# Attention products with v issued as quarter-array matmuls into two PSUM banks, probabilities copied whole, one visit moved by a place

## The chip, the cores and the metric

The kernel runs on one core of a Trainium2 chip. The metric is the device time of one execution in microseconds (us), lower is better; runs of the same program on the same chip are compared by their medians. Engine names are those of the profile: PE is the matrix engine (PEld its weight loads), DVE the vector engine, ACT the scalar engine, POOL the general engine, SP the queue that issues input transfers.

## The reference, cut to what matters

Chunked attention followed by a gated two-layer network:

```python
def _attn_ref(q, k, v, mem_k, mem_v):            # q, k, v: 4 x 8 x 768 x 64, 8 memory keys
    chunk, left_ctx, right_ctx = (32, 16, 8)
    for c in range(S // chunk):
        ...                                       # k_full, v_full: memory + 16 left + 32 own + 8 right = 64 keys
        scores = scale * np.matmul(q_c, k_full.transpose(0, 1, 3, 2))
        scores = scores - np.max(scores, axis=-1, keepdims=True)
        a = np.exp(scores)
        a = a / (np.sum(a, axis=-1, keepdims=True) + 1e-09)
        out[:, :, c_start:c_end] = np.matmul(a, v_full)

def _moe_ref(x, w_gate, w_val, w_out, rms_g):     # x: 3072 x 512, inner width 1536
    rms = np.sqrt(np.mean(x * x, axis=-1, keepdims=True) + 1e-06)
    xn = x / rms * rms_g
    g = xn @ w_gate
    silu = g * (1.0 / (1.0 + np.exp(-g)))
    val = xn @ w_val
    return (silu * val @ w_out)
```

## The kernel before

**Network.** The 3072 tokens are eight blocks of 384. For each block and each of 12 slices of the inner width (`f`), PE makes `pg` (gate, 12 matmuls of 128x128 weights on 384 columns), `pv` (value, 12 of the same) and adds to `po` (output, 9 matmuls on 512 columns). Each operand is split into a high and a low part, so that three matmuls stand for one. ACT and DVE turn `pg` and `pv` into `hh` and `hl`, the high and low part of the inner activations, that `moe_out` of that slice needs: tanh (`silu_a`), `silu_b` (in the first blocks after `gr`, a product of `pg` with the row scale), `moe_m` (`t<-t,pv`), `moe_hh`, `moe_hl`.

**Attention.** It is cut into 32 units: batch, half of the sequence, and a pair of heads. The first eight units, the first two blocks and the preparation of the weights run in a first part whose order is written out by hand (`ORDER`, up to about 150 us). What follows are seven segments: segment 0 finishes block 0 from slice 5 on, segments 1 to 6 do blocks 2 to 7. The other 24 units, twelve pairs, are done inside segments 0 to 5, in visits.

**Visits.** A segment has places ("gaps"): gap 2j stands behind `pg` of its j-th slice, gap 2j+1 behind `pv` of it; then comes `po` of the slice before. `VISITS` says at which gaps the generator `late_steps` advances: "v" is a visit, "n" one step of the norm that closes a block's input, "p" a visit's first half alone. Visit n does, for the pair of before (`old`): the transposes of the probabilities `pT` (`stage_p`, 6 matmuls), their copies to SBUF (`stage_c`; the tiles are named `pt` for even units and `qp` for odd ones, where q and the probabilities share a tile), the products with v (`stage_o`) and the copies into the block's input `xT` with their squares `sq` (`late_r`); for the pair of now (`cur`): the scores `s` (`stage_s2`, 48 small matmuls: 64 rows by 32 columns of the array each), the maximum `mx`, the difference, the exponential (`stage_m`, `stage_e`) and the normalisation `r`, `pe<-pe,r` (`stage_d`); and it issues the loads of the next pair. Every second visit closes a block: `late_n` splits the sum of squares into `sh` (ACT) and `sl` (DVE), and in the next "n" step PE sums them over the partitions (`ssum`). Twelve visits have products with v: two in segment 0 (gaps 5 and 9), two in each of segments 1 to 4 (gaps 5 and 17), and in segment 5 gap 5 and the pair of gaps 17 ("p") and 18.

**Products with v before.** The copies spread each unit's transposed probabilities into a tile twice as wide, zero elsewhere, so that one matmul serves two neighbouring chunks: all 128 rows of the array hold both chunks' keys (`v` of the pair of chunks), 64 columns, and 64 moving columns. That is 12 matmuls a unit, two units one after the other; the first unit's result goes to a bank of the pool `psa` (three banks in turn), the second's to the bank of `pv`. Each unit's copy is made in two halves, by ACT and by DVE.

**What sets the order.** PE's late instructions keep the program's order (`on_pe`). DVE's and ACT's order is set by the framework's scheduler from priorities, and each engine runs its list strictly in that order.

Of the kernel before, what the change touches and what calls it, by code (L numbers as in the profile page):

```python
# [8 lines left out]
F32 = mybir.dt.float32  # L9
# [4 lines left out]
AF = mybir.ActivationFunctionType  # L14
ALU = mybir.AluOpType
# [5 lines left out]
CH = 32  # L21
# [3 lines left out]
P = 128  # L25
NG = H // 2
HT = 384
NT = HT // P
NC = HT // CH
NJ = NC // 2  # L30
# [4 lines left out]
NE = NG * 2  # L35
WP = 2 * KC - LC - RC
KN, VN = NJ * WP, NJ * 2 * D
# [2 lines left out]
YMAX = 0x1DFE / 0x1000 * 2.0 ** -96  # L40


VISITS = (((1, "v"), (5, "v"), (9, "v"), (10, "n"), (11, "n"), (12, "n")),
# [27 lines left out]
def tile_kernel(ctx: ExitStack, tc: tile.TileContext, q, k, v, w_gate, w_val, w_out, rms_g, out):  # L71
    nc = tc.nc
    const = ctx.enter_context(tc.tile_pool(name="const", bufs=1))
    p1 = ctx.enter_context(tc.tile_pool(name="p1", bufs=1))
# [28 lines left out]
    def on_pe(ins):  # L103
        if pinned:
            tc.keep_in_program_order(ins)

    def psum_a(name):
        return psa.tile([P, 512], F32, name=name, tag="at")

    def psum_m(tag, name):  # L110
        return psm.tile([P, 512], F32, name=name, tag=tag)
# [4 lines left out]
    units = [(b, hf, g) for b in range(B) for hf in range(2) for g in range(NG)]  # L116
    st = {}
    pts = [early.tile([P, NT, 4, 2, CH], F32, name=f"pt{i}") for i in range(2)]
    late = {}

    def zeros(t):
        nc.gpsimd.memset(t, 0.0)
        return t

    def late_buffers(i):

        if i:
            t = p1.tile([P, HT + VN], F32, name="qp1", tag="A")
            late["q", 1], late["pt", 1] = t[:, 0:HT], zeros(t[:, HT:])
            late["kv", 1] = p1.tile([P, KN + VN], F32, name="kv1", tag="B")  # L130
        else:
            late["q", 0] = p1.tile([P, HT], F32, name="q0", tag="q")
            late["pt", 0] = zeros(p1.tile([P, VN], F32, name="pt0", tag="wy"))
            late["kv", 0] = p1.tile([P, KN + VN], F32, name="kv0", tag="ws")
        late["pt", i] = late["pt", i].rearrange("p (i a s q) -> p i a s q", i=NT, a=4, s=2)

    def load_qk(u):
        d = st.setdefault(u, {})
# [16 lines left out]

    def pt_of(u):

        return pts[u % 2] if u < NE else late["pt", u % 2]

    def copy(e, out, in_):  # L160
        if e == "a":
            return nc.scalar.copy(out, in_)  # L162
        if e == "g":
            return nc.gpsimd.tensor_copy(out=out, in_=in_)
        return nc.vector.tensor_copy(out=out, in_=in_)  # L165
# [37 lines left out]
    def stage_m(u):  # L203
        stage_ma(u)
        stage_mb(u)
# [20 lines left out]
    def stage_e(u):  # L226
        pe = st[u]["p"]
        nc.scalar.activation(pe, pe, AF.Exp, scale=0.125)

    def stage_d(u):  # L230
        stage_da(u)
        stage_db(u)
# [25 lines left out]
    def stage_p(u, tag=None):  # L258
        d = st[u]
        t = psum_m(tag, f"pT{u}") if tag else psum_a(f"pT{u}")  # L260
        pe = d["p"].rearrange("p j k -> p (j k)")
        for i in range(NT):
            on_pe(nc.tensor.transpose(out=t[:, i * P:(i + 1) * P], in_=pe[:, i * P:(i + 1) * P], identity=ident))  # L263
        d["t"] = t

    def stage_c(u):
        stage_ch(u, 0, "a")
        stage_ch(u, 1, "d")

    def stage_ch(u, hh, e):  # L270
        r = slice(64 * hh, 64 * hh + 64)
        t4 = st[u]["t"][:, 0:HT].rearrange("p (i a q) -> p i a q", i=NT, q=CH)
        copy(e, pt_of(u)[r, :, :, hh, :], t4[r])

    def stage_o(u, tag=None):

        pt, vw = pt_of(u), st[u]["v"]
        o = psum_m(tag, f"o{u}") if tag else psum_a(f"o{u}")
        for j in range(NJ):
            for hh in range(2):  # L280
                on_pe(nc.tensor.matmul(o[64 * hh:64 * hh + 64, j * D:(j + 1) * D], lhsT=vw[:, j, hh],  # L281
                                 rhs=pt[:, j // 2, 2 * (j % 2) + (hh ^ (u % 2 if u >= NE else 0))].rearrange("p c q -> p (c q)"),
                                 start=True, stop=True))
        st[u]["o"] = o[:, 0:HT]

    def late_r(u, x):

        g = units[u][2]
        o = st.pop(u)["o"]
        nc.scalar.copy(x[:, g], o)  # L290
        s = obuf(f"sq{u}")[:, 0:HT]
        nc.scalar.activation(s, x[:, g], AF.Square)
        if g:
            nc.vector.tensor_tensor(out=s, in0=s, in1=late["ss"], op=ALU.add)
        late["ss"] = s

    def late_n(x):

# [191 lines left out]
    def obuf(name):  # L490
        return p3.tile([P, DM], F32, name=name, tag="stg")
# [59 lines left out]
    def last_of(eng):  # L551
        return next(i for i in reversed(nc.cur_bb.bb.instructions) if i.engine == eng.engine)

    late_x = {}

    def late_steps():


        pairs = [(u, u + 1) for u in range(NE, len(units), 2)]
        for n in range(len(pairs) + 1):  # L560
            old = pairs[n - 1] if n else ()
            cur = pairs[n] if n < len(pairs) else ()
            new = pairs[n + 1] if n + 1 < len(pairs) else ()
            for u in old[0:1]:
                if u % NG == 0:
                    late_x["x"] = p1.tile([P, NKT, HT], F32, name="xT", tag="x")
            x = late_x.get("x")
            with tc.high_priority():
                for i, u in enumerate(old):
                    stage_p(u, None if i else "g")  # L570
                for u in old:
                    stage_c(u)
            if not cur:
                yield "p"
            with tc.high_priority():
                if cur:
                    stage_s2(cur)
                for u in cur:
                    stage_m(u)
                for u in cur:  # L580
                    stage_e(u)
                for i, u in enumerate(old):
                    stage_o(u, "v" if cur and i else None)
                for u in old:
                    late_r(u, x)
            norm = late_n(x) if n and n % 2 == 0 else ()
            if norm:
                with tc.high_priority():
                    next(norm)
            with tc.high_priority():  # L590
                for i, u in enumerate(cur):
                    if norm and i:
                        with tc.issue_after(last_of(nc.vector)):
                            stage_d(u)
                    else:
                        stage_d(u)
            for u in new:
                load_qk(u)
            for u in cur if n else ():
                load_v(u)  # L600
            yield "v"
            for _ in norm:
                yield "n"
# [10 lines left out]
    sq = [xq[:, i] for i in range(4)]  # L614
# [68 lines left out]
    def tok_o(n):  # L683
# [10 lines left out]
        P=lambda n: stage_p(n, "o0" if n < NG else None),  # L694
# [4 lines left out]
        g=tok_in("g"), v=tok_in("v"), p=tok_q("g"), q=tok_q("v"),  # L699
        r=tok_r, h=tok_h, i=tok_i, j=tok_j, k=tok_k, l=tok_l, o=tok_o,  # L700
# [5 lines left out]
    for tok in ORDER.split():  # L706
# [4 lines left out]
        e = tok[-1] if tok[1:] and tok[-1].isalpha() else ""  # L711
# [38 lines left out]

    xs = xs01[0]
    todo = late_steps()
    for sg, (blk, f0) in enumerate(segments):
        po = [psm_o(i) for i in range(NT)] if sg else sp["po", 0]
        last = sg == len(segments) - 1
        steps = {} if last else dict(VISITS[min(sg, 2) + (sg == len(segments) - 2)])

        def visit(gap):
            if gap in steps and next(todo, None) not in (steps[gap], None):
                raise AssertionError(gap)  # L760
        for f in range(f0, NF):
            g = moe_in("g", f, xs, last)
            visit(2 * (f - f0))
            out_ = lambda f=f, h=prev: moe_out(f - 1, h, po)
            if f == f0:
                out_ = lambda: None
                if sg == 0:

                    moe_out(NF - 1, prev, po1)
                    with tc.high_priority():  # L770
                        store(1, po1)
            vv = moe_in("v", f, xs, last)
            visit(2 * (f - f0) + 1)
            if f < NF - 1:
                out_()
                prev = moe_h(g, vv, blk)
            elif last:
                out_()
                finish(f, g, vv, po, blk)
            else:  # L780
                with tc.high_priority():
                    t = moe_t(g, vv, blk)
                xs = split_x(late_x["x"], t, out_, lambda h: moe_out(NF - 1, h, po))
        if sg == 0:
            behind.close()
        if not last:
            store(blk, po)
# [65 lines left out]
```

## Time and profile before

| what | value |
|---|---|
| median of 3 runs (lowest, highest) | 708.42 us (708.2, 708.72) |
| the profiled execution: its time, its span | 707.74 us, 705.9 us |
| busy: PE, PEld, DVE, ACT, POOL | 687.4, 636.3, 392.3, 261.4, 6.1 us |
| instructions | 13419 |
| products with v in the visits (L281) | 576 PE records, 12 visits |
| scores in the visits (L200) | 1152 PE records, 12 visits |

The span runs from the first to the last instruction; 1.84 us of the execution lie outside it. A row of the timeline gives the start, the duration, the engine, the line, the operation, `out<-in`, the array tile (rows*columns), the operand's shape and a count of merged records. A matmul's duration is its way through the array; how often matmuls can follow each other is read from the distance of their starts. A matmul on plain fp32 operands leaves two records, one on split operands (`xh`, `wh_g` and the like) one.

### The profile page before, as it was taken

What the parts mean: (1) busy time and instruction counts of PE and PEld (TensorE: products, weight loads), DVE (VectorE), ACT (ScalarE), POOL (GpSimd) and SP (SyncE); (2) the same over time, 40 slices, a digit from 0 to 9 for tenths busy, and PEclk for the clock granted to TensorE, in tenths of its full rate; (3) what the DMA queues carried; (4) which work ended last, traced back from release to release, by engine and by line L of the source; (5) the groups of instructions that cost most, each with busy time, mean ns of one, the idle gap of its engine ahead of it and who ended that gap; (6) DMA issues with size and microseconds to landing.
All of it is one profiled execution on the core that took longest, in us unless ns stands there. A gap on an engine that the chain in (4) does not pass through costs nothing.

```text
span 705.9 us, 13419 instructions
## 1 busy us (share of the span) xinstructions
PE 687.4 (97%) x5702; PEld 636.3 (90%) x5702; DVE 392.3 (56%) x780; ACT 261.4 (37%) x474; POOL 6.1 (1%) x14
## 2 busy tenths in 40 slices
PE   7899999999999999999999999999999999999997
PEld 6798898999989999999999999999999999999996
DVE  6789999857674327552383525735276532552222
ACT  4697987733333113331233313222133311331112
POOL 0010000000000000000000000000000000000000
PEclk8899999999999999999999999999999999999999
DMA  9644644333321103130021303013031100010001
GB/s 319 246 167 137 235 149 139 115 132 109 115 90 51 58 0 105 46 104 1 17 90 45 105 1 89 16 46 105 1 104 46 45 3 0 1 46 1 0 1 46
DMA packets 22620, 55.14 MB, mean 78 GB/s; under 512 B 2464, under 2 KB 6816, under 8 KB 22560
## 3 DMA queue, kind: packets, MB, share of 16 engines
q1 hardware_dynamic: 19824, 49.55, 20.9%
q10 hardware_dynamic: 2736, 4.72, 1.8%
q8 instruction: 45, 0.74, 0.5%
q14 instruction: 15, 0.12, 0.1%
HBM read 47.97 MB, written 6.29 MB: 77 GB/s over the span
## 4 chain that ended last, share of the span: by engine, by line
PE 88%; DVE 5%; ACT 4%; issue 1%; DMA 1%; POOL 0%; SPq 0%; DVEq 0%; ACTq 0%
PE pg L437 27%; PE pv L437 27%; PE po L487 27%; PE o L281 3%; PE pT L263 1%; ACT pt L162 1%; DVE pt L165 1%; DVE qp L165 1%; DMA k<-in_k_dram 1%; ACT ws L392 1%; ACT ws L381 1%; PE s L184 1%; PE ss L622 1%; ACT wy L382 1%; DVE xT L325 1%
## 5 line engine op out<-in xcount | busy, mean ns | idle before, releaser
L437 PE MATMUL pv<-xh,wh_v 128*128 128x384 f32 x384 | 130.1, 339 | 2.1 <-DVE t L458 2.1
L437 PE MATMUL pg<-xh,wh_g 128*128 128x384 f32 x384 | 130.5, 340 | 0.0
L437 PE MATMUL pv<-xh,wl_v 128*128 128x384 f32 x384 | 129.7, 338 | 0.5 <-DVE wl_v L408 0.5
L437 PE MATMUL pg<-xl,wh_g 128*128 128x384 f32 x384 | 129.8, 338 | 0.0
L437 PE MATMUL pg<-xh,wl_g 128*128 128x384 f32 x384 | 129.8, 338 | 0.0
L437 PE MATMUL pv<-xl,wh_v 128*128 128x384 f32 x384 | 129.6, 337 | 0.0
L162 ACT CAST hh<-t 128x384 fp32r<-128x384 f32 x89 | 45.8, 515 | 192.7 <-PE po L487 176.0
L487 PE MATMUL po<-wh_o,hh 128*128 128x512 f32 x285 | 113.9, 400 | 0.7 <-ACT hh L744 0.6
L487 PE MATMUL po<-wh_o,hl 128*128 128x512 f32 x285 | 112.6, 395 | 0.0
L487 PE MATMUL po<-wl_o,hh 128*128 128x512 f32 x285 | 112.3, 394 | 0.0
L455 DVE SCALAR_TENSOR_TENSOR t<-t,pg 128x384 f32<-128x384 f32 x72 | 39.9, 554 | 105.8 <-ACT t L451 105.7
L467 DVE TENSOR_TENSOR hl<-t,hh 128x384 fp32r<-128x384 f32 x89 | 49.5, 556 | 85.7 <-ACT hh L162 85.6
L458 DVE TENSOR_TENSOR t<-t,pv 128x384 f32<-128x384 f32 x95 | 52.7, 554 | 71.5 <-PE pv L437 70.2
L451 ACT ACTIVATE t<-pg 128x384 f32<-128x384 f32 x72 | 35.5, 493 | 120.2 <-PE pg L437 120.2
L437 PEld LDWEIGHTS pg<-xh,wh_g 128*128 128x128 f32 x384 | 72.3, 188 | 4.1 <-DVE gr L446 0.4
L437 PEld LDWEIGHTS pg<-xl,wh_g 128*128 128x128 f32 x384 | 72.3, 188 | 3.6
L437 PEld LDWEIGHTS pv<-xh,wh_v 128*128 128x128 f32 x384 | 72.0, 188 | 3.6 <-DVE t L458 1.8
L437 PEld LDWEIGHTS pv<-xh,wl_v 128*128 128x128 f32 x384 | 72.0, 188 | 0.8 <-DVE wl_v L408 0.8
L437 PEld LDWEIGHTS pg<-xh,wl_g 128*128 128x128 f32 x384 | 72.2, 188 | 0.0
L437 PEld LDWEIGHTS pv<-xl,wh_v 128*128 128x128 f32 x384 | 72.1, 188 | 0.1
L487 PEld LDWEIGHTS po<-wh_o,hl 128*128 128x128 f32 x285 | 53.6, 188 | 13.6 <-DVE hl L745 0.6
L487 PEld LDWEIGHTS po<-wh_o,hh 128*128 128x128 f32 x285 | 53.5, 188 | 10.7 <-ACT hh L744 1.6
(110 smaller groups left out, 717.2 us busy)
## 6 DMA issues: line engine op xcount, KB each, us to landing
kv<-in_v_dram SPq DMA_DIRECT2D x24, 384.0 KB, 5.6
kv<-in_k_dram SPq DMA_DIRECT2D x24, 312.0 KB, 4.2
out_dram<-ob ACTq DMA_DIRECT2D x18, 256.0 KB, 2.1
ws<-in_moe_w_gate_dram SPq DMA_DIRECT2D x4, 1024.0 KB, 4.9
ws<-in_moe_w_val_dram SPq DMA_DIRECT2D x4, 1024.0 KB, 5.0
ws<-in_moe_w_out_dram SPq DMA_DIRECT2D x4, 1024.0 KB, 5.0
q<-in_q_dram SPq DMA_DIRECT2D x20, 192.0 KB, 3.1
vw<-in_v_dram SPq DMA_DIRECT2D x8, 384.0 KB, 7.3
```

Of the source, the lines that this page charges most:

```text
L162: return nc.scalar.copy(out, in_)
L165: return nc.vector.tensor_copy(out=out, in_=in_)
L184: nc.tensor.matmul(s[a:a + CH, o:o + KC], lhsT=d["q"][r, c * CH:c * CH + CH], rhs=k[r], start=True, stop=True)
L263: on_pe(nc.tensor.transpose(out=t[:, i * P:(i + 1) * P], in_=pe[:, i * P:(i + 1) * P], identity=ident))
L281: on_pe(nc.tensor.matmul(o[64 * hh:64 * hh + 64, j * D:(j + 1) * D], lhsT=vw[:, j, hh], rhs=pt[:, j // 2, 2 * (j % 2) + (hh ^ (u % 2 if u ...
L325: nc.vector.scalar_tensor_tensor(out=x[:, kt], in0=x[:, kt], scalar=rg[:, kt:kt + 1], in1=r, op0=ALU.mult, op1=ALU.mult)
L437: on_pe(nc.tensor.matmul(ps[:, 0:HT], lhsT=weight(a, n, f, kt), rhs=xs[c][:, kt], start=kt == 0 and i == 0, stop=kt == NKT - 1 and i == 2))
L451: nc.scalar.activation(t, g, AF.Tanh, scale=0.5)
L455: nc.vector.scalar_tensor_tensor(out=t, in0=t, scalar=1.0, in1=g, op0=ALU.add, op1=ALU.mult)
L458: nc.vector.tensor_tensor(out=t, in0=t, in1=vv, op=ALU.mult)
L467: nc.vector.tensor_tensor(out=hl, in0=t, in1=hh.bitcast(F32), op=ALU.subtract)
L487: on_pe(nc.tensor.matmul(po[i], lhsT=h[a][:, i * P:(i + 1) * P], rhs=weight(c, "o", f), start=f == 0 and n == 0, stop=f == NF - 1 and n == 2))
```

## The change

Four edits that go together:

- `stage_o2` in place of two `stage_o`: each product with v is cut into the two chunks that shared the rows. A matmul has 64 rows (one chunk's keys), 64 columns and 32 moving columns; chunks on the upper rows write the bank `oe` (from `psa`), those on the lower rows the bank `oo`. A pair of units takes 48 matmuls in place of 24, the four quarters of the array in turn.
- `stage_c` copies a unit's transposed probabilities in one piece of 128x384, ACT for the even unit, DVE for the odd one; the tiles are half as wide and the two zeroing instructions on POOL go.
- `late_r` copies the pair's results from the two banks, each copy holding every second chunk of both units, into `xT`, then makes both squares.
- The third visit of segment 0 moves from gap 9 to gap 8, the norm steps from 10, 11, 12 to 9, 10, 11. Which bank the first transposes and `oo` take now follows the gap (`lent["even"]`): at an odd gap `pg`'s and `pv`'s as before, at an even one `pv`'s and `pg`'s.

```diff
-VISITS = (((1, "v"), (5, "v"), (9, "v"), (10, "n"), (11, "n"), (12, "n")),
+VISITS = (((1, "v"), (5, "v"), (8, "v"), (9, "n"), (10, "n"), (11, "n")),
...
     def stage_c(u):
-        stage_ch(u, 0, "a")
-        stage_ch(u, 1, "d")
+        copy("da"[u % 2 == 0], late["pt", u % 2], st[u]["t"][:, 0:HT])
...
+    def stage_o2(pair, tag):
+
+        st["o2"] = o2 = [psum_a(f"oe{pair[0]}"), psum_m(tag, f"oo{pair[0]}") if tag else psum_a(f"oo{pair[0]}")]
+        for j in range(NJ):
+            for n, u in enumerate(pair):
+                pt = late["pt", u % 2].rearrange("p (j e q) -> p j e q", j=NJ, e=2)
+                for cp in range(2):
+                    r, o = slice(64 * cp, 64 * cp + 64), (NJ * n + j) * CH
+                    for hh in range(2):
+                        on_pe(nc.tensor.matmul(o2[cp][64 * hh:64 * hh + 64, o:o + CH], lhsT=st[u]["v"][r, j, hh],
+                                               rhs=pt[r, j, hh ^ u % 2], start=True, stop=True))
...
+        xc = x[:, g:g + 2].rearrange("p g (j c q) -> p g j c q", c=2, q=CH)
+        for cp in range(2):
+            nc.scalar.copy(xc[:, :, :, cp], o2[cp][:, 0:HT].rearrange("p (g j q) -> p g j q", g=2, q=CH))
...
-                    stage_p(u, None if i else "g")
+                    stage_p(u, None if i else "gv"[lent["even"]])
...
-                for i, u in enumerate(old):
-                    stage_o(u, "v" if cur and i else None)
-                for u in old:
-                    late_r(u, x)
+                if old:
+                    stage_o2(old, "vg"[lent["even"]] if cur else None)
+                    late_r(old, x)
```

PE at the visit of gap 5 in segment 0, before: the last score rows (`s`), the two units' products (`pt` is the even unit's, `qp` the odd one's probabilities), then the output matmuls of the network.

```order
L200 MATMUL s_1960<-kv_1718,q_1715 32x64 x2
L200 MATMUL s_1961<-kv_1742,qp_1740 32x64 x2
L281 MATMUL o_2020<-pt_1716,kv_1718 64x64 x12
L281 MATMUL o_2033<-qp_1740,kv_1742 64x64 x12
L487 MATMUL po_808<-wh_o_1082,hh 128x512
```

PE at the same place now, the last of the 24 rows of products:

```order
L289 MATMUL oe_2016<-pt_1716,kv_1717 64x32 x2
L289 MATMUL oo_2017<-pt_1716,kv_1717 64x32 x2
L289 MATMUL oe_2016<-qp_1739,kv_1740 64x32 x2
L289 MATMUL oo_2017<-qp_1739,kv_1740 64x32 x2
L498 MATMUL po_808<-wh_o_1082,hh 128x512
```

The place in PE's order is the same; 24 matmuls of 64 moving columns have become 48 of 32, the two units' interleaved, so that the second half of the first eight matmuls already needs the odd unit's copy.

DVE in the visit that closes block 2's input (segment 0, third visit), before: from the first unit's sum `r` to the row that PE's `ssum` waits for, `sl`.

```order
L250 TENSOR_REDUCE r_2271<-pe_2225 128x6
L294 TENSOR_TENSOR sq_2260<-sq_2260,sq_2050 128x384
L251 TENSOR_SCALAR r_2271<-r_2271 128x6
L252 RECIPROCAL r_2271<-r_2271 128x6
L256 TENSOR_TENSOR pe_2225<-pe_2225,r_2271 128x384
L246 MEMSET pe_2229 64x8
L294 TENSOR_TENSOR sq_2264<-sq_2264,sq_2260 128x384
L250 TENSOR_REDUCE r_2277<-pe_2229 128x6
L467 TENSOR_TENSOR hl<-t,hh 128x384
L251 TENSOR_SCALAR r_2277<-r_2277 128x6
L302 TENSOR_TENSOR sl<-sq_2264,sh 128x384
```

The same stretch of DVE's order now:

```order
L245 TENSOR_REDUCE r_2300<-pe_2230 128x6
L246 TENSOR_SCALAR r_2300<-r_2300 128x6
L247 RECIPROCAL r_2300<-r_2300 128x6
L251 TENSOR_TENSOR pe_2230<-pe_2230,r_2300 128x384
L241 MEMSET pe_2234 64x8
L245 TENSOR_REDUCE r_2306<-pe_2234 128x6
L246 TENSOR_SCALAR r_2306<-r_2306 128x6
L247 RECIPROCAL r_2306<-r_2306 128x6
L251 TENSOR_TENSOR pe_2234<-pe_2234,r_2306 128x384
L305 TENSOR_TENSOR sq_2290<-sq_2290,sq_2070 128x384
L305 TENSOR_TENSOR sq_2293<-sq_2293,sq_2290 128x384
L313 TENSOR_TENSOR sl<-sq_2293,sh 128x384
```

Both sums of squares, and with them `sl`, have moved behind the whole normalisation of the second unit. The visits at gap 17 of segments 1 to 4 have the same new order.

PE around `ssum` in segment 0, before (gap 10) and now (gap 9), the last row of the matmul group ahead and what follows:

```order
L437 MATMUL pg<-xh_145,wl_g_1488 128x384
L306 MATMUL ssum<-sh,one 128x384
L306 MATMUL ssum<-sl,one 128x384
L437 MATMUL pv<-xh_145,wh_v_1489 128x384
L437 MATMUL pv<-xl_146,wh_v_1489 128x384
```

```order
L448 MATMUL pv<-xh_145,wl_v_1093 128x384
L317 MATMUL ssum<-sh,one 128x384
L317 MATMUL ssum<-sl,one 128x384
L498 MATMUL po_808<-wh_o_1088,hh 128x512
L498 MATMUL po_808<-wl_o_1089,hh 128x512
```

Before, `po` of a slice and `pg` of the next stood between the visit's products and `ssum`; now only the slice's `pv` does.

More of the change, by code (lines that the diff above doesn't have):

```diff
@@ L119, in tile_kernel @@
     late = {}
-    def zeros(t):
-        nc.gpsimd.memset(t, 0.0)
-        return t
     def late_buffers(i):
         if i:
-            t = p1.tile([P, HT + VN], F32, name="qp1", tag="A")
-            late["q", 1], late["pt", 1] = t[:, 0:HT], zeros(t[:, HT:])
+            t = p1.tile([P, 2 * HT], F32, name="qp1", tag="A")
+            late["q", 1], late["pt", 1] = t[:, 0:HT], t[:, HT:]
             late["kv", 1] = p1.tile([P, KN + VN], F32, name="kv1", tag="B")
@@ L132, in late_buffers @@
             late["q", 0] = p1.tile([P, HT], F32, name="q0", tag="q")
-            late["pt", 0] = zeros(p1.tile([P, VN], F32, name="pt0", tag="wy"))
+            late["pt", 0] = p1.tile([P, HT], F32, name="pt0", tag="wy")
             late["kv", 0] = p1.tile([P, KN + VN], F32, name="kv0", tag="ws")
-        late["pt", i] = late["pt", i].rearrange("p (i a s q) -> p i a s q", i=NT, a=4, s=2)
     def load_qk(u):
@@ L156, in pt_of @@
     def pt_of(u):
-        return pts[u % 2] if u < NE else late["pt", u % 2]
+        return pts[u % 2]
     def copy(e, out, in_):
@@ L281, in stage_o, with late_r @@
                 on_pe(nc.tensor.matmul(o[64 * hh:64 * hh + 64, j * D:(j + 1) * D], lhsT=vw[:, j, hh],
-                                 rhs=pt[:, j // 2, 2 * (j % 2) + (hh ^ (u % 2 if u >= NE else 0))].rearrange("p c q -> p (c q)"),
+                                 rhs=pt[:, j // 2, 2 * (j % 2) + hh].rearrange("p c q -> p (c q)"),
                                  start=True, stop=True))
         st[u]["o"] = o[:, 0:HT]
[L286 to L295, printed above, removed]
+    def stage_o2(pair, tag):
[8 more added lines that the diff above has]
+                                               rhs=pt[r, j, hh ^ u % 2], start=True, stop=True))
+    def late_r(pair, x):
+        g = units[pair[0]][2]
+        o2 = st["o2"]
+        for u in pair:
+            st.pop(u)
+        xc = x[:, g:g + 2].rearrange("p g (j c q) -> p g j c q", c=2, q=CH)
+        for cp in range(2):
+            nc.scalar.copy(xc[:, :, :, cp], o2[cp][:, 0:HT].rearrange("p (g j q) -> p g j q", g=2, q=CH))
+        for i in range(g, g + 2):
+            s = obuf(f"sq{i}")[:, 0:HT]
+            nc.scalar.activation(s, x[:, i], AF.Square)
+            if i:
+                nc.vector.tensor_tensor(out=s, in0=s, in1=late["ss"], op=ALU.add)
+            late["ss"] = s
     def late_n(x):
@@ L554, in tile_kernel @@
     late_x = {}
+    lent = {}
     def late_steps():
@@ L758, in visit @@
         def visit(gap):
+            lent["even"] = gap % 2 == 0
             if gap in steps and next(todo, None) not in (steps[gap], None):
```

## The prediction

> **What bounds the kernel now.** First I read the busy shares and the shares of the chain that ended last, then the waits of PE, then PE's timeline at one visit.
>
> ```profile
> PE 687.4 (97%) x5702; PEld 636.3 (90%) x5702; DVE 392.3 (56%) x780; ACT 261.4 (37%) x474; POOL 6.1 (1%) x14
> PE 88%; DVE 5%; ACT 4%; issue 1%; DMA 1%; POOL 0%; SPq 0%; DVEq 0%; ACTq 0%
> PE o L281 <- DVE qp L165: 2.3, 11, 0.3
> ```
>
> PE is busy for 97% of the span and 88% of the ending chain. So a change counts by what it does to the distance between PE's starts. The third row is the one wait of PE that recurs: eleven times the products with v waited for DVE's copy of the second unit's probabilities. A wait is counted from the modelled end of the matmuls ahead, so the distance of starts says more. PE at the visit at gap 5 of segment 0:
>
> ```profile
> 170.12 0.82 PE L263 MATMUL pT<-ident,pe 128*128 128x128 f32 x6
> 170.87 0.25 PE L200 MATMUL s<-kv,q 64*32 64x64 f32 x2
> ...
> 171.81 0.23 PE L200 MATMUL s<-kv,qp 64*32 64x64 f32 x2
> 172.30 0.92 PE L281 MATMUL o<-pt,kv 128*64 128x64 f32 x24 [0.26 <-DVE qp L165]
> 173.05 0.87 PE L281 MATMUL o<-qp,kv 128*64 128x64 f32 x24
> 173.85 0.50 PE L487 MATMUL po<-wh_o,hh 128*128 128x512 f32 x1
> ```
>
> The visit costs PE 3.73 us (170.12 to 173.85): transposes 0.75, scores 0.96 (96 records, 10 ns apart), a hole of 0.47 to 172.30, products 1.55 (48 records, 31 to 32 ns apart).
>
> **Part 1, the copies.** The hole comes from the copies:
>
> ```profile
> 170.71 0.47 ACT L162 COPY pt<-pT 64x384 f32<-64x384 f32 x1 [1.33 <-PE pT L263]
> 171.21 0.56 DVE L165 COPY pt<-pT 64x384 f32<-64x384 f32 x1 [0.33 <-ACT pt L162]
> 171.69 0.55 DVE L165 COPY qp<-pT 64x384 f32<-64x384 f32 x1
> ```
>
> DVE's first half waits for ACT's first half, and its second ends at 172.24. Now ACT makes one copy, 170.71 to 171.18, and DVE one. A copy's time goes with its 384 columns, so halving the rows saved nothing and a whole one costs the same 0.47 and 0.55. DVE's can start when the sixth transpose is through (170.12 + 0.82 = 170.94, and some 0.06 for the signal) and ends at 171.55, before the scores' last start at 171.81. The hole closes except for the change of array tiling, which the trace shows elsewhere:
>
> ```profile
> 159.29 0.23 PE L200 MATMUL s<-kv,qp 64*32 64x64 f32 x2
> 159.45 0.44 PE L437 MATMUL pg<-xh,wh_g 128*128 128x384 f32 x1
> ```
>
> From the last scores to a full-array matmul pass 0.16 us. I take the products to start at 171.97: gain 0.33 a visit. Bounds: 0.26 if they wait for the scores' way through the array (171.81 + 0.23), 0.47 if nothing is left. Twelve copies each leave DVE and ACT; neither bounds PE there. If DVE's copy came 0.2 us later, the cover by the scores would be gone and each 0.1 us would cost 1 us in ten visits.
>
> **Part 2, the products.** No row shows a 64x64 tile with 32 moving columns. 96 records take the place of 48. From below: before, each half of the array took a record every 62 ns (31 for two halves); with half the moving columns 31 ns for each quarter and 24 records, 0.75 us; the scores' pace, 96 records in eight tiles, gives 0.96. From above: if records only follow each other as the products' did, 96 x 31 ns = 2.98 us. Between them, a quarter must load 64 weight columns for each record, and with only 32 columns to move behind it the load may bind. A row where loads have almost nothing behind them:
>
> ```profile
> 41.79 1.40 PE L622 MATMUL ss<-onef,xq 128*128 128x1 f32 x12
> 43.12 1.62 PE L281 MATMUL o<-pt,vw 128*64 128x64 f32 x48
> ```
>
> Twelve loads of 128 columns took 1.33 us, 111 ns each; 64 columns are then about 55 ns, and 24 in each quarter 1.33 us. I take 1.3, nearest to this row: gain 0.25 a visit. The small gain is the price of twice as many loads. The Trainium skill, "TensorE: Matmul & The Clock Gate", section "Wait — 56ns, not 53.3ns?", says that starts never follow each other closer than about 25 ns however few columns move; by that the products would be an estimated 96 x 25 ns = 2.4 us. The trace disagrees for tiles side by side: the scores' starts are 10 ns apart.
>
> **Part 3, the closing visits of segments 1 to 4.** The change puts `sl` behind the second unit's normalisation, and behind `sl` queue `hl` and `t<-t,pv`; PE's `ssum` waits for it. The new chain on DVE, paced by these rows:
>
> ```profile
> 172.28 1.02 DVE L211 TENSOR_REDUCE mx<-s 128x6 f32<-128x384 f32 x2
> ...
> 174.49 0.55 DVE L250 TENSOR_REDUCE r<-pe 128x6 f32<-128x384 f32 x1
> 175.07 0.17 DVE L251 TENSOR_SCALAR r<-r 128x6 f32<-128x6 f32 x1
> ...
> 175.58 0.54 DVE L256 TENSOR_TENSOR pe<-pe,r 128x384 f32<-128x384 f32 x1
> ...
> 176.04 0.54 DVE L250 TENSOR_REDUCE r<-pe 128x6 f32<-128x384 f32 x1
> ```
>
> ```profile
> 193.00 0.56 DVE L294 TENSOR_TENSOR sq<-sq,sq 128x384 f32<-128x384 f32 x1
> 193.60 0.51 ACT L301 CAST sh<-sq 128x384 fp32r<-128x384 f32 x1 [0.61 <-DVE sq L294]
> 194.48 0.55 DVE L302 TENSOR_TENSOR sl<-sq,sh 128x384 fp32r<-128x384 f32 x1
> 194.62 0.33 PE L306 MATMUL ssum<-sh,one 128*128 128x384 f32 x1
> 195.09 0.44 PE L306 MATMUL ssum<-sl,one 128*128 128x384 f32 x1
> 195.37 0.34 PE L437 MATMUL pv<-xh,wh_v 128*128 128x384 f32 x1
> ```
>
> Counted from the first transpose: scores through at 1.69 + 0.23 + 0.05 = 1.97; `mx` to first `r` 2.21; first `r` to its `pe` 1.09, to the second `r` 0.46, again 1.09 and 0.46 to the first `sq`; 0.58 to the second, which needs it; 0.60 to `sh`; 0.54 to `sl`; 0.61 until PE runs on it. Sum 9.61 us. PE's arrival, from the visit at gap 17 of segment 1:
>
> ```profile
> 265.34 0.82 PE L263 MATMUL pT<-ident,pe 128*128 128x128 f32 x6
> ...
> 269.01 0.50 PE L487 MATMUL po<-wh_o,hh 128*128 128x512 f32 x1
> ...
> 271.23 0.33 PE L437 MATMUL pg<-xh,wh_g 128*128 128x384 f32 x1
> ...
> 273.34 0.34 PE L437 MATMUL pv<-xh,wh_v 128*128 128x384 f32 x1
> ...
> 275.63 0.34 PE L306 MATMUL ssum<-sl,one 128*128 128x384 f32 x1
> ```
>
> Before, PE came 10.29 us after the first transpose (visit 3.67, `po` 2.22, `pg` 2.11, `pv` the same, the first `ssum` row 0.18); now 10.29 - 0.33 - 0.25 = 9.71. That clears `sl` by 0.1 us: no stall, but no further gain either. Faster products than 1.2 us would be given back here, in four visits. `hl`, one DVE start after `sl`, is ready at about 10.1 and needed at 10.3.
>
> **Part 4, the moved visit.** In segment 0 the chain of 9.61, plus 0.1 for `silu_b` which now stands ahead of `mx`, begins where PE ends `pg` of the fifth slice:
>
> ```profile
> 184.51 0.34 PE L437 MATMUL pv<-xh,wh_v 128*128 128x384 f32 x1
> ...
> 205.66 0.40 PE L487 MATMUL po<-wh_o,hl 128*128 128x512 f32 x1
> 206.68 0.50 PE L487 MATMUL po<-wh_o,hh 128*128 128x512 f32 x1 [0.62 <-ACT hh L744]
> ```
>
> `sl` lets PE go at 184.51 + 9.71 = 194.2. PE itself, with only `pv` between, is there after 3.67 - 0.58 + 2.11 + 0.18 = 5.38, at 189.9, and stands for 4.3 us; before it stood 0.3 (195.09 - 194.62 - 0.18). From there: 0.28 for `ssum`, `po` 2.1 (2.22 less the change of tiling that no longer stands ahead of it), `pg` 2.1. The next `pv` starts at 198.7 against 195.37, 3.3 later, with this visit's own gain already in it. Given back: the norm ends a step earlier, and the hole of 1.02 between the 205.66 and 206.68 rows shrinks to the usual 0.23. Net +2.5 us. The loads of the visit (six on SP's queue, whose order does not change) go out a place earlier and have over 10 us until the next visit; the zeroing on POOL was on no chain. Both cost nothing.
>
> **Sum.** Ten visits with scores and products (six plain, four closing) at 0.33 + 0.25: -5.8. The last visit, products alone: -0.25. Segment 0's third visit: +2.5. Together -3.55 us against the profiled execution's 707.74: 704.2. The median of the runs is 0.68 above that execution, so 704.9.
>
> **The rivals.**
> - *Halving the moving columns brings nothing* (records every 62 ns in a quarter as before): products 1.55 us as before, the gain is the hole alone, -3.3 + 2.5, time 707.6. For it: a tile's records lay 62 ns apart in the products and 80 ns in the scores (0.96 us for 12 in each of eight tiles). Against it: both had 64 columns to move. The Trainium skill, "TensorEngine Tiling (Array Packing)", section "Instruction Overhead", states about 60 cycles for each matmul, by which few columns cost as much as 60; whether that binds fp32's two records no run here shows.
> - *Slower: the quarters don't overlap across the row halves.* Records then follow at up to 31 ns, products 2.98 us, +1.1 a visit in ten, +1.4 in the last, +2.5: 723. From about 17 ns a record on (1.62 us a visit) the change no longer gains. For it: no 64x64 tile in the trace. Against it: the scores mix row halves at 10 ns. By the 25 ns that the Trainium skill, "TensorE: Matmul & The Clock Gate", states, the estimate is 717; it is a case within this one, and the scores' rows speak against it as well.
> - *The products run at the scores' pace*, 0.96 us: six visits gain 0.92, four are held by `sl` at 0.68, the last 0.6, then +2.5: -6.3, 702.1.
> - *The change does not move the norm's path as I read it*: `ssum` finds `sl` ready or the stall is hidden. Segment 0 then gains 0.58 and 0.79, the sum is -7.4, 701.0. Against it: DVE runs in the order shown.
>
> **How the numbers follow.** Chances: forecast 0.52, scores' pace 0.16, no stall 0.09, columns bring nothing 0.12, slower quarters 0.11. The range leaves out the last and reaches from 701.0 to the columns rival with the scatter of runs, 708.0. What counts as no change is within 0.2%, 1.4 us: 707.0 to 709.8. The first three cases are faster (0.77), the columns rival the same (0.12), the last slower (0.11).
>
> **What would show it.** The wait of `o` for `qp` gone from PE's waits. The products as 96 records within 1.2 to 1.4 us, starting 0.1 to 0.2 us behind the last scores. One wait of PE at `ssum` of about 4 us near 190, and none over 0.3 us in the later closing visits. The 0.62 wait for `hh` gone. The forecast is wrong if the records lie 20 ns or more apart, or if every closing visit stalls.

## The result and the profile after

The changed kernel takes 718.54 us (median of 4 runs, 718.18 to 719.06), the kernel before beside it 708.45 (708.2 to 708.72): a ratio of 1.0143, 95% interval 1.0125 to 1.016. The forecast, 704.9 us, is wrong in sign. The profiled execution's span is 716.4 us against 705.9.

From the page of the changed kernel: busy times, the shares of the chain that ended last, and the queue that brings PE's instructions (packets, MB, share):

```profile
PE 693.5 (97%) x6278; PEld 642.4 (90%) x6278; DVE 388.1 (54%) x768; ACT 257.5 (36%) x462; POOL 4.6 (1%) x12
PE 71%; issue 1%; DVE 1%; ACT 0%
q8 instruction: 49, 0.80, 0.5%
```

The wait of the products for `qp`, 2.3 us in eleven visits before, is gone from the list of PE's waits. In its place stand two rows for the products (us in total, times, longest):

```profile
PE oe L289 <- issue: 4.9, 5, 1.6
PE oo L289 <- issue: 3.4, 2, 1.8
```

"Issue" means that PE waited for nothing that the profile shows: no semaphore, no transfer of data. Seven waits in all. The profile before has one such wait of PE, and it lies outside the visits: in the first part, up to 26.8 us, inside a group of matmuls with one moving column.

```profile
PE ss L622 <- issue: 2.1, 1, 2.1
```

PE's timeline at the visit of gap 5 in segment 0 shows where one of the seven lies:

```profile
168.82 0.82 PE L258 MATMUL pT<-ident,pe 128*128 128x128 f32 x6
...
170.50 0.23 PE L195 MATMUL s<-kv,qp 64*32 64x64 f32 x2
170.67 0.25 PE L289 MATMUL oe<-pt,kv 64*64 64x32 f32 x2
...
171.46 0.22 PE L289 MATMUL oo<-pt,kv 64*64 64x32 f32 x1
173.45 0.24 PE L289 MATMUL oo<-pt,kv 64*64 64x32 f32 x1 [1.77 <-issue]
...
174.01 0.26 PE L289 MATMUL oo<-qp,kv 64*64 64x32 f32 x2
174.21 0.50 PE L498 MATMUL po<-wh_o,hh 128*128 128x512 f32 x1
```

The products begin 1.85 us after the first transpose, as forecast. Then PE stands from 171.46 to 173.45, in the middle of one product: the first of its two records has run, the second comes 1.99 us later. The visit at gap 17 of segment 3 does the same work without a stop:

```profile
398.26 0.82 PE L258 MATMUL pT<-ident,pe 128*128 128x128 f32 x6
...
399.95 0.23 PE L195 MATMUL s<-kv,qp 64*32 64x64 f32 x2
400.11 0.25 PE L289 MATMUL oe<-pt,kv 64*64 64x32 f32 x2
...
401.49 0.23 PE L289 MATMUL oo<-qp,kv 64*64 64x32 f32 x2
401.64 0.50 PE L498 MATMUL po<-wh_o,hh 128*128 128x512 f32 x1
```

That visit costs 3.38 us against 3.67 before. All twelve, from the first transpose (in the last, the first product) to the next wide matmul:

| visit at (after) | 169 | 186 | 228 | 273 | 315 | 357 | 398 | 439 | 481 | 522 | 565 | 615 |
|---|---|---|---|---|---|---|---|---|---|---|---|---|
| before, us | 3.73 | 3.67 | 3.67 | 3.67 | 3.67 | 3.67 | 3.67 | 3.67 | 3.67 | 3.67 | 3.67 | 1.55 |
| after, us | 5.39 | 5.22 | 5.23 | 3.99 | 3.96 | 3.38 | 3.38 | 3.38 | 3.38 | 4.89 | 5.03 | 1.53 |

Seven of eleven full visits have a stop. Without stops the eleven would take 37.2 us, 3.2 less than before; the stops bring 10.0.

A second loss follows from the first. The stretch view, in which the figure behind POOL is the granted clock, at a stretch after the second stop and at a later one:

```profile
192.40:195.80 3.40, 3.06 (x11) 2.55 (x9) 2.63 (x7) 1.63 (x4) 0.00 (x0) 0.50 0.88 304
199.00:202.40 3.40, 3.40 (x21) 3.40 (x20) 3.30 (x8) 0.56 (x2) 0.00 (x0) 1.00 0.00 0
```

PE ran at half clock for 3.41 us, 11 matmuls in place of 21. The late part has four such stretches, from 175.3, 192.4, 233.3 and 571.3 us, each after a stop of 1.6 to 2.0 us. Before, there is none between 33 us and the last 1.1 us of the span. What one costs is read where it stands alone: from the visit at 228 to the next pass 44.69 us against 41.69, of which the stop explains 1.85 less 0.29, so 1.44 are left; from 565 to the last products 49.52 against 46.59, which leaves 1.57.

The account, against the 10.5 us by which the span grew: visits without their stops -3.2, stops +10.0, four stretches at half clock an estimated +6.0 (1.5 each, from the two read alone), the first part of the kernel -1.3 (the first late transposes start at 168.82 against 170.12). The remaining -1.0 is not told apart; the hole at segment 0's end, which shrank from 1.02 us to the usual 0.23, belongs to it.

### The profile page after: what moved, and what is told of

Same layout as the page of the kernel before. It is cut to its first block, busy times and chain, and to the rows that moved or that the text cites. A ratio compares the mean times of both kernels' runs of the same rounds, so it can differ in the third digit from the quotient of the medians.

```text
span 716.4 us, 14544 instructions
## 1 busy us (share of the span) xinstructions
PE 693.5 (97%) x6278; PEld 642.4 (90%) x6278; DVE 388.1 (54%) x768; ACT 257.5 (36%) x462; POOL 4.6 (1%) x12
## 4 chain that ended last, share of the span: by engine, by line
PE 71%; issue 1%; DVE 1%; ACT 0%
PE po L498 22%; PE pg L448 22%; PE pv L448 21%; PE oe L289 2%; PE s L195 1%; PE pT L258 1%; PE oo L289 1%; PE ssum L317 0%; PE po L526 0%; DVE xT L336 0%; DVE sq L305 0%; DVE sl L313 0%; DVE t L466 0%; ACT hh L755 0%; ACT sh L312 0%
## 5 line engine op out<-in xcount | busy, mean ns | idle before, releaser
L498 PE MATMUL po<-wl_o,hh 128*128 128x512 f32 x285 | 113.9, 400 | 0.0
```

Of the source, the lines that this page charges most:

```text
L498: on_pe(nc.tensor.matmul(po[i], lhsT=h[a][:, i * P:(i + 1) * P], rhs=weight(c, "o", f), start=f == 0 and n == 0, stop=f == NF - 1 and n == 2))
```

## The experiments

PE's instructions were counted from the start of the program in each trace: a weight load, a matmul and a semaphore instruction of PE's queue each as one (a product on plain fp32 is two loads and two matmuls). All seven stops fall behind instruction 193 modulo 256 (193 or 194 where a weight load that stands together with its matmul is counted in). The instruction queue moves packets of 16 KB, 45 before and 49 after, for 11472 and 12624 instructions on PE: 255 and 258 a packet. And in each of the seven visits a packet of this queue starts 2.4 to 2.8 us before PE goes on, and takes 0.98 to 1.39 us itself. So theory I: PE's instructions come in blocks of 256, and when a block is used up faster than the next comes in, PE stands. Transposes, scores and products are 12 + 192 + 96 instructions before and 12 + 192 + 192 after. Rival Q: the stop belongs to quarter matmuls or to writing two banks by turns. Rival S: the time is lost in the chain on DVE behind the normalisation.

**Each visit cut in two.** In the changed kernel:

```diff
-VISITS = (((1, "v"), (5, "v"), (8, "v"), (9, "n"), (10, "n"), (11, "n")),
-          ((5, "v"), (17, "v"), (19, "n"), (20, "n"), (21, "n")),
+VISITS = (((1, "v"), (5, "s"), (6, "v"), (7, "s"), (8, "v"), (10, "n"), (11, "n"), (12, "n")),
+          ((5, "s"), (6, "v"), (15, "s"), (16, "v"), (19, "n"), (20, "n"), (21, "n")),
...
+            if old and cur:
+                yield "s"
...
-                    stage_o2(old, "vg"[lent["even"]] if cur else None)
+                    stage_o2(old, None)
```

> The changed kernel with each late visit cut in two: transposes, probability copies and scores at one gap of the sweep, the products by row halves and the evictions at the next gap, with a group of wide matmuls between them. Theory I (PE's instructions come in blocks of 256, and a block that is used up in less than about 3.5 us leaves PE without instructions, because transposes, scores and products together issue 396 in 2.9 us): the 256 instructions now last longer than 3.5 us everywhere, no stop inside the products, each visit 1.85 + 1.53 = 3.38 us, 0.29 less than the kernel before's 3.67 in 11 visits, no half-clock stretch after 150 us: 704.0 to 706.0 us. Rival Q (the stop belongs to the quarter matmuls or to writing two banks by turns): seven stops of 0.6 to 2 us remain inside the products, 715 us or more. Rival S (the time is lost where the normalization waits for VectorE): the stops stay or go without the time following, 712 us or more.

Measured: 706.63 us against 708.56, ratio 0.9973 (0.9956 to 0.9989). No stop in any of the twelve visits, though all quarter matmuls are there. PE's timeline at the first split products:

```profile
176.22 0.25 PE L289 MATMUL oe<-pt,kv 64*64 64x32 f32 x2
...
177.59 0.23 PE L289 MATMUL oo<-qp,kv 64*64 64x32 f32 x2
177.75 0.44 PE L448 MATMUL pv<-xh,wh_v 128*128 128x384 f32 x1
```

1.53 us, and 1.85 for the first half: the 3.38 of the visits without a stop, and no late stretch at half clock. The blocks that hold these bursts now last 4.4 us or more. Q and S fall. The gain is smaller than the 2.5 to 4.5 us expected, because a second break in the wide work costs time of its own. Behind the scores the first wide matmul is 0.33 us ahead of the second, where the usual distance is 0.23:

```profile
171.80 0.50 PE L498 MATMUL po<-wh_o,hh 128*128 128x512 f32 x1
172.13 0.40 PE L498 MATMUL po<-wl_o,hh 128*128 128x512 f32 x1
```

and the last `pg` ahead of the products is 0.27 (175.95 to 176.22) where 0.18 is usual: some 0.2 us for the extra break, against the 0.29 gained.

**More instructions in the kernel before.** Two thirds of a visit's scores issued a second time:

```diff
-        for i in range(NT):
+        for i in [*range(NT), *((0, 1) if pair[0] > NE else ())]:
```

> The kernel before with 32 of the 96 score matmuls of a visit issued a second time, in every visit from the second on (the same operands, the same result), so that a visit issues 428 instructions on PE instead of 300, of which no one has a quarter tile and two banks in the products. Added work alone: 32 matmuls of about 10 ns are 0.32 us in 11 visits, 3.5 us: 712 us. Theory I: besides that, PE stops for 0.3 to 2 us in at least three of the eleven visits, each time at the same place counted in PE instructions modulo 256 as in the changed kernel (193 or 194), 714 to 722 us. Rival Q: no stop, 711 to 712.5 us.

(A visit has 48 score matmuls, 96 records; the text's 32 of 96 are 32 of these 48.) Measured: 721.79 us, ratio 1.0188 (1.0159 to 1.0217). Eight of eleven visits stop, all behind instruction 193 modulo 256, four inside the scores and four inside the old products with 64 columns. From PE's timeline, one of each kind:

```profile
172.50 0.22 PE L200 MATMUL s<-kv,qp 64*32 64x64 f32 x1
174.76 0.21 PE L200 MATMUL s<-kv,qp 64*32 64x64 f32 x1 [2.04 <-issue]
...
359.32 0.34 PE L281 MATMUL o<-pt,kv 128*64 128x64 f32 x4
361.02 0.80 PE L281 MATMUL o<-pt,kv 128*64 128x64 f32 x20 [1.37 <-issue]
```

A visit without a stop takes 4.02 us, 0.35 more than before: the scores take 0.63 us longer, of which 0.28 falls into the old hole. The stops add 10.4 us. This kernel has no quarter tile and no `oe`, `oo`: Q is excluded.

**The move of the third visit alone, in the kernel before.**

```diff
-VISITS = (((1, "v"), (5, "v"), (9, "v"), (10, "n"), (11, "n"), (12, "n")),
+VISITS = (((1, "v"), (5, "v"), (8, "v"), (9, "n"), (10, "n"), (11, "n")),
...
-                    stage_p(u, None if i else "g")
+                    stage_p(u, None if i else "gv"[lent["even"]])
```

(The bank of the second product tile follows in the same way.)

> The kernel before with the move of the third visit of segment 0 from place 9 to place 8 alone, products and copies as before. By the prediction's fourth step: a stall of about 4.3 us at the sum of squares in segment 0 and 1.0 us less at the segment's end, 711 to 712 us. Theory I: the instruction count is unchanged and the blocks are used up as slowly as before, so the move is worth only what the two holes are: between -1.0 and +0.9 us, 707.5 to 709.3 us.

Measured: 711.08 us, ratio 1.003 (1.001 to 1.0051), within the 711 to 712 us of the prediction's fourth step and outside what theory I allowed. No stop at a block's end. The time agrees with the fourth step only as a sum: in place of one stall of 4.3 us at `ssum`, PE waits in two places of the moved visit:

```profile
186.26 0.23 PE L200 MATMUL s<-kv,qp 64*32 64x64 f32 x2
187.40 0.92 PE L281 MATMUL o<-pt,kv 128*64 128x64 f32 x24 [0.91 <-DVE qp L165]
...
191.00 0.34 PE L437 MATMUL pv<-xh,wl_v 128*128 128x384 f32 x1
192.82 0.44 PE L306 MATMUL ssum<-sh,one 128*128 128x384 f32 x1 [1.48 <-ACT sh L301]
193.67 0.44 PE L306 MATMUL ssum<-sl,one 128*128 128x384 f32 x1 [0.41 <-DVE sl L302]
```

The products come 0.7 us later than elsewhere, and PE stands at `ssum` for 1.48 and 0.41 us; a stretch at half clock follows (3.41 us from 194.67). So in the kernel before the move costs 2.5 us (0.7 to 3.6 by the interval).

**The block boundaries shifted.** In the changed kernel 24 warm-up matmuls more, in two places of the hand-written first part:

```diff
-... M0 S1 a0 E0 U7 M1 a1 E1 d0 S2 Z J n0 ...
+... M0 S1 W12 a0 E0 U7 M1 a1 E1 d0 S2 W12 Z J n0 ...
```

> The changed kernel with 24 warm-up matmuls more in the first part, 96 instructions on PE, far ahead of the first late visit: every later instruction stands 96 places further in its block of 256. Nothing else is changed. Theory I: the stops move to other visits. By the index of the block's end within the products, visits 2 to 5 of the late part and those at 480 and 440 us have none, the one at 356 and 398 us gain stops of 0.5 to 2 us, the one at 522 us keeps about 0.6 to 1.5 us and that at 565 us at most 0.6; the stops' sum falls from 9.9 to about 6 us, and 710 to 714 us follow. Rival Q: the stops stay in the same visits with the same lengths, 718.5 us and up to 1 us more for the warm-up.

Measured: 717.0 us, ratio 1.0114 (1.0074 to 1.0154). The stops moved, as I says: the five visits from 169 to 309 us have none and take 3.38 to 3.40 us (3.96 to 5.39 with their stops), and the visits at 392, 437 and 481 us, free before, now take 5.36, 5.19 and 4.98. The last two of these I had reckoned free, so my count of where a boundary falls was off there. All five stops are behind instruction 193 modulo 256, and one has left the attention work altogether:

```profile
353.97 0.39 PE L498 MATMUL po<-wh_o,hh 128*128 128x512 f32 x1
354.87 0.50 PE L498 MATMUL po<-wl_o,hh 128*128 128x512 f32 x1 [0.50 <-issue]
```

Here PE stands between two matmuls of the network, after the visit. The time lies above the expected 710 to 714 us. The stops' sum came to 6.9 us in place of about 6, and with no stop in the third visit the wait of the prediction's fourth step came out:

```profile
188.48 0.33 PE L448 MATMUL pv<-xh,wl_v 128*128 128x384 f32 x1
192.21 0.69 PE L317 MATMUL ssum<-sh,one 128*128 128x384 f32 x1 [3.40 <-ACT sh L312]
```

**Copies by unit in the kernel before.**

```diff
-        stage_ch(u, 0, "a")
-        stage_ch(u, 1, "d")
+        for hh in range(2):
+            stage_ch(u, hh, "da"[u % 2 == 0])
```

> The kernel before with the probabilities copied by unit instead of by row halves: ScalarE copies both halves of the even unit, VectorE both of the odd one, as the change does, but into the block form with zeros, and the products stay 48 matmuls of 128 rows. The third visit stays at place 9. In the kernel before, VectorE's first half copy starts only when ScalarE's ends, and its second ends 0.43 us after the scores. Theory I: the hole of 0.43 closes, a visit's 300 instructions take 3.24 us instead of 3.67 and some blocks of 256 are used up faster than before, so at most four visits may get a stop of up to 0.5 us: 703 to 706 us, faster than the kernel before by 0.4 to 0.8 per cent. If the hole was itself the time in which PE's next instructions came in, stops take its place in most visits: 707 to 709 us.

Measured: 708.86 us against 708.48, ratio 1.0003 (0.999 to 1.0017). The hole did not close (a visit takes 3.78 us), and not for want of instructions: it starts at any count modulo 256. DVE's two copies and PE's first product in one visit:

```profile
308.68 1.12 DVE L165 COPY qp<-pT 64x384 f32<-64x384 f32 x2
310.06 0.92 PE L281 MATMUL o<-pt,kv 128*64 128x64 f32 x24 [0.32 <-DVE qp L165]
```

A product that reads `pt` waits for the last copy into `qp`, though ACT had finished `pt` at 309.31. Neither theory had this; it led to the last experiment.

**The split without the new products.** The kernel before with the visits cut as in the first experiment.

> The kernel before with its visits cut in two as in the first experiment (products and copies as before): the copies have a group of wide matmuls as cover. If the products by row halves bring nothing by themselves (1.53 us against 1.55 from their start to the next group), this gives the same as the first experiment within 0.15 per cent: 705.5 to 707.5 us beside a kernel before of 708.5. If the prediction's 0.25 us for the products was right, it is 2.7 us slower than the first experiment.

Measured: 706.53 us, ratio 0.997 (0.9955 to 0.9985), the same as with the new products. In PE's timeline:

```profile
176.73 0.92 PE L281 MATMUL o<-pt,kv 128*64 128x64 f32 x24
177.47 0.87 PE L281 MATMUL o<-qp,kv 128*64 128x64 f32 x24
178.27 0.44 PE L437 MATMUL pv<-xh,wh_v 128*128 128x384 f32 x1
```

1.54 us against 1.53. Cutting the products by row halves brings next to nothing by itself.

**The new products with half copies.** In the changed kernel:

```diff
-        copy("da"[u % 2 == 0], late["pt", u % 2], st[u]["t"][:, 0:HT])
+        for hh, e in enumerate("ad"):
+            r = slice(64 * hh, 64 * hh + 64)
+            copy(e, late["pt", u % 2][r], st[u]["t"][r, 0:HT])
```

> The changed kernel with the probabilities copied by row halves, ScalarE one and VectorE the other, as in the kernel before; the products by row halves and the move to place 8 stay. Theory I: the products wait 0.2 to 0.45 us for the copies, in which the next block comes closer, so the stopped visits keep their length (the stop gets shorter by the wait) and only the four or five visits without a stop get longer: plus 1 to 2 us against the changed kernel, 718.5 to 721 us. If the stop were set by the products themselves, all eleven visits get longer, 721 to 723.5 us.

Measured: 721.6 us, ratio 1.0189 (1.0158 to 1.0221). By the time alone the second expectation (721 to 723.5) is met and the first missed, but the four runs spread from 719.16 to 725.25, over both. The trace, of a run of 719.75 us, speaks for the first: the wait for DVE's copy is back in all eleven visits,

```profile
PE oe L291 <- DVE qp L160: 3.0, 11, 0.9
```

the four visits without a stop take 3.65 us, 0.27 more, and the six with a stop take 4.27 to 5.34 and differ from the changed kernel's by -0.26 to +0.31. The eleven together are 1.2 us longer, inside what I said (1 to 2). One visit that had a stop, at 273 us, has only 0.12 of it left.

**The third visit back at place 9, in the changed kernel.**

> The changed kernel with the third visit of segment 0 back at place 9. In segment 0 the sum of squares of the closing visit then comes one group later, as in the kernel before, with the hole of 1.0 us at the segment's end back. In the changed kernel the move cost little because PE stood 1.8 us inside the products first. Theory I: stops at the ends of blocks stay, in the third visit at another place of the block; 716 to 719.5 us. By the prediction's fourth step alone: 3.3 us less than the changed kernel, 715 us.

Measured: 717.06 us, ratio 1.013 (1.0105 to 1.0155). The stops lie in the same visits as in the changed kernel but for the third, which has none and takes 3.38 us. At `ssum` PE still stands once:

```profile
196.15 0.44 PE L317 MATMUL ssum<-sh,one 128*128 128x384 f32 x1 [1.30 <-ACT sh L312]
```

So the stops are the loss; what the move adds here is within the scatter (1.013 against 1.0143, with overlapping intervals).

**The banks of the products exchanged, in the kernel before.**

```diff
-                    stage_o(u, "v" if cur and i else None)
+                    stage_o(u, "v" if cur and not i else None)
```

> The kernel before with one thing changed: of the two product tiles of a visit the even unit's goes to the bank of pv and the odd unit's to the next of the three rotating banks, instead of the other way round. Order of instructions, copies and products are the same. The fifth experiment showed that the products on pt start only when VectorE's last copy, that of qp, has ended. Theory B: the even unit's product tile takes the rotating bank that held the odd unit's transposes, so its first product waits for the last copy out of that bank; with the banks exchanged it waits for the copies of pt alone, which end 0.2 us before the scores do, and the hole of 0.43 closes to about 0.15: 3.38 us a visit, 11 times 0.28 = 3.1 us less, 705.4 us beside 708.5, range 704.5 to 706.3. With 300 instructions a visit and 15.6 ns for each instruction of the products the blocks of 256 are used up in 2.3 us or more, so that by the stops seen so far none is longer than 0.1 us here. Rival: the wait is the copy of pt itself, or a stop of PE's instructions takes the hole's place: 708 to 709 us.

Measured: 706.39 us against 709.04, ratio 0.9967 (0.9953 to 0.9982): faster than both kernels with one word. The order of the instructions is untouched. DVE's last copy and PE's products in one visit, from two timelines:

```profile
306.96 0.56 DVE L165 COPY qp<-pT 64x384 f32<-64x384 f32 x1
```

```profile
307.29 0.92 PE L281 MATMUL o<-pt,kv 128*64 128x64 f32 x24
308.04 0.87 PE L281 MATMUL o<-qp,kv 128*64 128x64 f32 x24
308.84 0.50 PE L487 MATMUL po<-wh_o,hh 128*128 128x512 f32 x1
```

The first product now starts before the copy of `qp` ends (307.52), 1.85 us after the first transpose, and a visit takes 3.40 us, one 3.46, as expected (3.38). Theory B holds: with three rotating banks, the transposes of the odd unit, two tiles of scores and then the even unit's products take turns, so the products get the bank that the odd unit's copies still read. The gain is 2.6 us in place of 3.1; PE stands 0.75 us between the two `ssum` matmuls of segment 0 (193.07 to 193.82), which it reaches earlier now. No stop in any visit.

**How fast a block may be used up.** From all these traces, the time from the first matmul of a block of 256 to its last within the late part. In the changed kernel the seven blocks that were used up in 1.6 to 1.9 us all ended in a stop; the next, 3.0 us, did not. In the kernel before the three fastest took 2.4 to 2.5 us, with the banks exchanged 2.1 to 2.3, none with a stop. So the 3.5 us in theory I's first wording was too much. The time of the block alone isn't the whole rule either: a block of 1.53 us in the second experiment and one of 1.64 in the eighth, both of segment 0's third visit, had no stop, and one of 2.76 us in the shifted kernel had one.

What decides is how long ago the packet started. Taken in order, each packet belongs to one block's end. After 150 us the eleven traces have 410 block ends. The 32 that PE reached 0.3 to 2.0 us after their packet's start are the 32 stops, and PE went on 2.18 to 2.80 us after that start; those that it reached 2.37 us after it or later have no "issue" wait, and the one between, at 2.09, waited 0.11 us. The two short blocks without a stop fit: their packets had started 4.7 and 2.6 us before their ends. The packet is on record for 0.9 to 1.4 us of this time; what fills the other 1.2 to 1.6 us, and what starts the packet, was not settled.

## Why the prediction was wrong, point by point

- **What bounds the kernel** (PE's starts): right, and it is why a loss in PE's supply shows in full.
- **Part 1, the copies.** Forecast: the products start at 1.85 us after the first transpose, DVE's copy is not waited for. Both came out. Two flaws: the 0.33 us came from the first visit; the other ten gained 0.27 to 0.28 (they started at 2.12 to 2.13 before). And the cause I gave, the length of DVE's copy, is half of it: the exchange of banks shows that the copy of the odd unit need not have been waited for at all.
- **Part 2, the products.** The mis-sized term of the sum: 1.3 us forecast, 1.53 measured, against 1.55 before. The records do overlap across the quarters, 14.4 ns apart (1.38 us from the first start to the last, where the row of loads gave 1.33), so the rival of quarters that don't overlap is excluded, and that its estimate of 717 us at 25 ns a record lies near the measured time is chance. What I left out is the change back to full tiles, about 0.15 us, which the 1.55 of before held as well (1.40 from the first start to the last). The last visit, the products alone:

```profile
614.97 0.25 PE L289 MATMUL oe<-pt,kv 64*64 64x32 f32 x2
...
616.34 0.23 PE L289 MATMUL oo<-qp,kv 64*64 64x32 f32 x2
616.50 0.44 PE L448 MATMUL pv<-xh,wh_v 128*128 128x384 f32 x1
```

  In effect the rival "halving the moving columns brings nothing" was right on this term.
- **Part 3, the closing visits of segments 1 to 4.** No stall at `ssum`: none there in PE's waits. Where no stop disturbs (398 to 439 us), that stretch takes 41.23 us against 41.62 before.
- **Part 4, the moved visit.** Forecast: PE stands 4.3 us at `ssum`. In the changed kernel it stood under 0.9:

```profile
194.71 0.53 PE L448 MATMUL pv<-xh,wl_v 128*128 128x384 f32 x1
195.58 0.53 PE L317 MATMUL ssum<-sh,one 128*128 128x384 f32 x1 [0.34 <-ACT sh L312]
196.17 0.44 PE L317 MATMUL ssum<-sl,one 128*128 128x384 f32 x1
```

  But only because PE had already lost 1.8 us inside this visit's products and ran at half clock (the 0.53 of these rows, 0.34 elsewhere), while ACT and DVE went on. In the shifted kernel, without that stop, it stood 3.4. The mechanism was right, its size 0.9 us too large, and it was hidden by the larger loss; the hole at segment 0's end went as forecast.
- **The step that failed is the sum.** It had no term for what 96 more instructions a visit ask of PE's supply, and no rival named it. In its place the runs showed stops of 10.0 us and, behind four of them, half clock for some 6 us more. The page of before showed the queue that brings the instructions (45 packets, 0.74 MB), the list of PE's waits of before held a stop of the same kind (`ss`, 2.13 us up to 26.8 us, also behind instruction 193 modulo 256, 2.5 us after its packet's start), and the prediction counted records where it should have counted instructions too: a visit of 396 in 3.38 us, where before it was 300 in 3.67. Of the signs that it named for being wrong none came: the records lie 14.4 ns apart, and the later closing visits don't stall. The Trainium skill, "Runtime: NRT & Kernel Launch", section "Instruction fetch mechanics", states that each engine's instructions are refilled in blocks of 256 while the current one runs, and that crossing a boundary is mostly hidden. The traces agree on the blocks (32 late stops in five kernels, every one behind instruction 193 modulo 256) and on most boundaries (32 of the changed kernel's 39 after 150 us cost nothing that shows), but seven of its boundaries, all inside a burst of small matmuls, cost 0.5 to 2.0 us each, and in the other kernels up to 2.3.

Without the stops the products and copies would have been worth 0.29 us a visit, nearly all of it from the products' earlier start, less what the moved visit costs. The exchange of two banks gives 0.27 of it with none of the added instructions.

## What to carry to other kernels

Where small matmuls follow each other at 5 to 10 ns an instruction, count instructions as well as time: about 256 of them in less than 2 us mostly left PE without any here, and an "issue" wait in the middle of a uniform run, always at the same count modulo 256, is the sign of it. Put wide matmuls between two such bursts, or keep the instructions few; cutting a matmul into smaller tiles pays only if its time falls by more than the added instructions cost; here it did not fall (1.53 us against 1.55). When a product waits for a copy that it doesn't read, look at which buffer its result goes to before touching the copy.

## What the runs showed of the hardware that was not expected

- A short stop can cost twice. In the changed kernel PE was granted half its clock for a stretch of 3.41 us after stops of 1.57 to 1.99 us, with 1.4 to 1.6 us lost in the two that could be read alone; in the shifted kernel a stop of 1.54 us was followed by one, and one of 1.62 was not. The Trainium skill, "TensorE: Matmul & The Clock Gate", section "Why this matters for your kernels", has the clock fall at idle gaps of more than about 3 us. Here half of that was enough.
- The length of a stop does not follow from how fast its block was used up: blocks of 1.57 and 1.71 us ended in stops of 0.56 and 1.99 us. PE went on 2.4 to 2.8 us after the start of the packet in all seven, and 2.18 to 2.80 in all 32.
- A change of tiling is not free in either direction: a break in the wide work costs about 0.2 us beside the matmuls in it.
- The first part of the kernel, which only the shifted kernel alters, took a different time in each profile: the first late scores start between 157.0 and 158.7 us, where the better versions gain 1.9 to 2.6 us in all. Stops of the same kind are part of it (the one near 25 us took 2.13 us in the kernel before and 0.34 in the changed one); the rest is open.
